# A fused attention and mixer kernel: the first 750 steps of the work issued in one written order on all five engines

## The chip, the cores and the metric

The kernel runs on one core of one Trainium2 chip. The metric is the device time of one execution in microseconds. The five engines that the text speaks of are PE (TensorE: matmuls and transposes), ACT (ScalarE), DVE (VectorE), POOL (GpSimd) and SP (SyncE, which only issues DMAs). Each works off its own instructions in the order in which they stand.

## The reference, cut to what matters

Linear attention over 8 batches, 8 heads, 576 tokens and 64 channels, and behind it a low-rank mixing over tokens and a two-layer MLP over channels, all in float32 accuracy. U, V, w_ch1 and w_ch2 arrive as float64.

```
phi(x):  proj = x @ w_phi                      # 64 -> 128
         proj -= max(abs(proj), axis=-1)
         return concat(exp(proj), exp(-proj))  # 256 features
q_p, k_p = phi(q), phi(k)
kv  = einsum('bhsf,bhsd->bhfd', k_p, v);  z = sum(k_p, axis=2)
x   = (q_p @ kv) / (q_p @ z + 1e-6)            # -> (8, 576, 512)
u   = x + ((x.T @ U) @ V).T                    # rank 32 over the 576 tokens
out = u + maximum(u @ w_ch1, 0) @ w_ch2        # 512 -> 2048 -> 512
```

## The kernel before, in words

**Pairs.** Attention is done in 32 pairs, (b, j), each two heads of a batch b, 512 tokens in the main part and 64 in a tail. A pair loads raw k and q (256 KB each) and the values, transposes both on PE (tiles T and tT), copies them from PSUM on ACT (T, tail_T; L393 to L399), multiplies by w_phi (pk and pkt for k, pq for q), forms the features (a maximum on DVE for k, on POOL for q, a subtraction on DVE, two exponentials on ACT), takes the kv product (36 matmuls into kv_ps, L549 and L559) and the output (xp, L577 and L584), and divides on DVE into x. From batch 2 on (pairs 8 and later) the operands are split into a rounded part and a remainder (`stack`, ACT L350 and DVE L351; pkt at L471), and w_phi is split into w_hl (L100 and L101).

**Tokens.** When a batch's four pairs are done, x is split into xs (ACT L656, DVE L657), multiplied by U into pp (`down`, L670), by V into vp (`up`, L686) and added to x, which is stored. U and V are converted from float64 in the kernel (u_st, v_st).

**Mixers.** There are eight mixers, one for each batch, and a ninth for the tails. A mixer transposes u (pt, L702) and splits it into uT_hi and uT_lo (L280 and L281), and then does 34 chunks: `hidden(f)` is 12 matmuls (L717) and a relu on ACT, `add(f)` is 4 matmuls in mixer 0 and 12 in the others (L748). One hidden chunk stands ahead of its add.

**Weights.** w_ch1 and w_ch2 come as 32 blocks of 512 KB of float64 words. A block is loaded by SP into one of four staging buffers (tag "wide", NW = 4) and converted to float32 by ACT (L141 and L147) and DVE: a mask (L144), a shift (L149), a combination (L152) and a join (L156). The mask, the shift and the combination read the staging buffer; after the last of them and ACT's L141 the buffer is free for a later load. A block of w_ch1 is then split into w_hi (ACT, L239) and w_lo (DVE, L246); those of w_ch2 are split in mixer 1, where they are first needed in two parts (`split_w2`, ACT L255 and DVE L256).

**The order around the change.** `early()` writes out the eight pairs of batches 0 and 1, the tokens of batch 0 and mixer 0, in the order of its code, helper by helper. A pair's step such as `whole_k` issues its matmuls, its DVE and its ACT instructions in one piece; `uv` converts U and V in four pieces; `conv(n)` converts n blocks; `chunk(n, blocks)` issues n chunks of mixer 0 and so many blocks. Mixer 0 has 23 of its chunks in `early()`. `keep_busy(n)` issues n matmuls of zeros (28 in all). PE, ACT, DVE and POOL follow this order; SP's is made by the scheduler. After that `ordered()` goes on with the pairs, chunk by chunk, and there only PE's order is written.

Of the kernel before, what the change touches and what calls it, by code (L numbers as in the profile page):

```python
# [21 lines left out]
HP = 64  # L22


@with_exitstack
def tile_kernel(
# [66 lines left out]

    def split_w():

        if not w_split:
            src = wide("w_src", (F,))
            load_w_phi(src)
            w_hl = const.tile([P, 2, F], F32R, tag="w_phi", name="w_hl")
            nc.vector.tensor_copy(out=w_hl[:, 0, :], in_=src)  # L100
            nc.vector.tensor_sub(w_hl[:, 1, :], src, f32(w_hl[:, 0, :]))  # L101
            w_split.append(w_hl)
        return w_split[0], w_split[0][:, 0, :], w_split[0][:, 1, :]
# [31 lines left out]
    def convert(st, a, b_, between=None):  # L135

        n = st.shape[1]
        hi_w = st[:, :, 1]
        halves = st.rearrange("p n w -> p (n w)").bitcast(U16).rearrange("p (n h) -> p n h", h=4)
        bh = b_.bitcast(U16).rearrange("p (n h) -> p n h", h=2)  # L140
        nc.scalar.activation(out=bh[:, :, 0], in_=halves[:, :, 1], func=AF.Copy, scale=2.0 ** -13)  # L141
        if between is not None:
            between()
        nc.vector.tensor_scalar(  # L144
            out=bh[:, :, 1], in0=halves[:, :, 3], scalar1=0x7FF0, scalar2=None,
            op0=ALU.bitwise_and)
        nc.scalar.activation(  # L147
            out=bh[:, :, 1], in_=bh[:, :, 1], func=AF.Relu, scale=8.0, bias=e_bias)
        nc.vector.tensor_scalar(  # L149
            out=a, in0=hi_w, scalar1=3, scalar2=0x7FFFF8,  # L150
            op0=ALU.logical_shift_left, op1=ALU.bitwise_and)
        nc.vector.scalar_tensor_tensor(  # L152
            out=a, in0=hi_w, scalar=-0x80000000, in1=a, op0=ALU.bitwise_and, op1=ALU.bitwise_or)

    def join(a, b_):
        nc.vector.tensor_tensor(out=a, in0=a, in1=b_, op=ALU.add)  # L156

    def staged(name, n):

        t = wide(name, (512, 2), I32)  # L160
        a, b_ = (t[:, 256 + 128 * i:256 + 128 * (i + 1), :].rearrange("p n w -> p (n w)")[:, 0:n]
                 for i in range(2))

        def go():
            convert(t[:, 0:n, :], a, b_)
            join(a, b_)
            return f32(a)

        return t[:, 0:n, :], go

    def uv_parts():
        st, go = staged("u_st", (NT + 1) * R)
        sv = st.rearrange("p (t r) w -> p t r w", r=R)
        nc.sync.dma_start(
            out=sv[:, 0:NT], in_=U[0:SM].rearrange("(p t) r w -> p t r w", t=NT))
        for g in range(2):
            nc.sync.dma_start(out=sv[g * ST:(g + 1) * ST, NT], in_=U[SM:S])
        cs3 = (slice(0, SM // 2), slice(SM // 2, SM), slice(SM, S))  # L180
        v_st = []
        for cs in cs3:
            sv, sgo = staged(f"v_st{cs.start}", cs.stop - cs.start)
            for g in range(4):
                nc.sync.dma_start(out=sv[g * R:(g + 1) * R], in_=V[:, cs])
            v_st.append(sgo)
        yield
        u_f = go().rearrange("p (t r) -> p t r", r=R)
        nc.vector.memset(f32(u_all[:, NT:NT + 2]), 0.0)
# [3 lines left out]
        for pr, to, of in parts:  # L193
# [5 lines left out]
        for cs, go in zip(cs3, v_st):  # L199
            yield  # L200
            v_f = go()
            vm = v_all[:, cs]
            if cs.stop <= SM:
                ps_ = slice(cs.start // NT, cs.stop // NT)
                v_f = v_f.rearrange("r (p t) -> r t p", t=NT)
                vm = v_all[:, 0:SM].rearrange("r (t p) -> r t p", t=NT)[:, :, ps_]
            nc.vector.tensor_copy(out=vm, in_=v_f)
            lo = slice(3 * R, 4 * R)
            nc.vector.tensor_sub(vm[lo], v_f[lo], f32(vm[lo]))


# [3 lines left out]
    AHEAD = 4  # L215
    loaded, begun, ended = [], [], [0]

    def load_block():
        i = len(loaded)
        f, m = i // 2, i % 2 + 1  # L220
        fs = slice(f * P, (f + 1) * P)
        st = wide(f"w{m}_{f}", (C, 2), I32)
        if m == 1:
            nc.sync.dma_start(
                out=st.rearrange("p (c n) w -> p c n w", c=NCC),
                in_=w1[:, fs].rearrange("(c p) n w -> p c n w", c=NCC))
        else:
            nc.sync.dma_start(out=st, in_=w2[fs])
        loaded.append(st)
# [29 lines left out]
    def conv(n=1):  # L259

        for _ in range(n):
            while len(loaded) < min(len(begun) + AHEAD, NB):
                load_block()
            some = ended[0] < len(begun)
            if len(begun) < NB:
                i = len(begun)
                f, m = i // 2, i % 2 + 1
                at = NFC + (f + 1 if m == 2 else (f + 2) % (NFC + 1))
                b_ = const.tile([P, C], I32, tag=f"wh{m}_{f}", name=f"w_b{m}_{f}")
                r = const.tile([P, C], F32, tag=f"wl{at}", name=f"w_r{m}_{f}")  # L270
                convert(loaded[i], r.bitcast(I32), b_, merge_block if some else None)
                begun.append((f, m, b_, r))
            elif some:
                merge_block()
            if some:
                end_block()


    def split_t(src, dst_hi, dst_lo):
        nc.scalar.copy(out=dst_hi, in_=src)  # L280
        nc.vector.tensor_sub(dst_lo, src, f32(dst_hi))  # L281

# [7 lines left out]
    home_of = {("xs1", t): homes[t] for t in range(NT + 1)}  # L290
# [15 lines left out]
    class Pair:  # L306


        def __init__(self, b, j):
            self.b, self.h0, self.nm, self.par = b, 2 * j, f"{b}_{j}", j % 2  # L310
            self.split = b >= SPLIT
            self.free = b * NPAIR + j <= NPAIR
            self.tail = slice((b % 2) * ST, (b % 2 + 1) * ST)
            nm, hs = self.nm, slice(self.h0, self.h0 + 2)
            self.raw = []
            for n, src in enumerate((k, q)):
                if b == 0:
                    m = home(("raw", j, n), (2, NT // 2, 2 * D), f"raw{nm}_{n}")
                else:
                    m = raw.tile(  # L320
                        [P, 2, NT // 2, 2 * D], F32, tag="raw", bufs=2, name=f"raw{nm}_{n}")
                nc.sync.dma_start(
                    out=m.rearrange("p h s e -> p h (s e)"),
                    in_=src[b, hs, 0:SM, :].rearrange("h (p t) d -> p h (t d)", t=NT))
                self.raw.append(m)

            if b == 0:
                self.t_r = home(("t_r", j), (2 * D,), f"t_r{nm}")
            else:
                self.t_r = raw.tile([P, 2 * D], F32, tag="t_r", bufs=1, name=f"t_r{nm}")  # L330
# [5 lines left out]
        def ps(self, name, late=False):  # L336
            return ps(f"{name}{self.nm}", "o" if late and self.free else "at")
# [10 lines left out]
        def stack(self, src, dst):  # L348

            nc.scalar.copy(out=dst[0:D], in_=src)  # L350
            nc.vector.tensor_sub(dst[D:2 * D], src, f32(dst[0:D]))  # L351
# [13 lines left out]
        def transpose_both(self):  # L365
# [11 lines left out]
            self.pT = []  # L377
            for n in self.order():
# [9 lines left out]
        def order(self):  # L388
            return (1, 0) if self.b == 0 else (0, 1)
# [435 lines left out]
    def early(x, xt):  # L825
# [15 lines left out]
        for i in range(NPAIR - 1):  # L841
# [12 lines left out]
            if i == 2:  # L854
                tk.down(0)
# [184 lines left out]
```

## Time and profile before

| | us |
|---|---|
| median of 3 runs | 1186.24 |
| lowest and highest | 1183.31, 1186.37 |
| the profiled execution, its own time | 1184.01 |
| its span, first to last instruction | 1182.1 |
| PE busy in the span | 1134.0 (96%) |
| DVE busy | 655.9 (55%) |
| ACT busy | 531.9 (45%) |
| POOL busy | 153.5 (13%) |
| mean granted clock of TensorE | 0.982 |

1.9 us of the execution lie outside the span. The first hidden matmul of mixer 0 starts at 88.15 us, that of mixer 1 at 245.81. In a row of the timeline stand the start, the busy time, the engine, the line, the operation, the output and inputs without their numbers, and the count; in brackets the idle time of the engine before it and what ended that. In a row of the waits stand who waited, whom for, the total in us, the times and the longest.

### The profile page before, as it was taken

The numbers are of one execution on the slowest core, as the hardware profiler recorded it, in microseconds if no ns is written. First come the engines' busy times: TensorE is split into PE (matmuls) and PEld (weight loads), VectorE is DVE, ScalarE is ACT, GpSimd is POOL, SyncE is SP. The second block draws the span as 40 slices with busy tenths as digits, with TensorE's granted clock in tenths as the row PEclk, the third lists the DMA queues.
The fourth block names the chain that finished last, engine by engine and source line by source line (L and its number), as shares of the span: only waits on it lengthen the run. The fifth ranks groups of instructions, "written<-read, shape, count | busy, mean of one in ns | idle before, by whom it ended". The sixth has DMA issues, their size and how long they took to land.

```text
span 1182.1 us, 22322 instructions
## 1 busy us (share of the span) xinstructions
PE 1134.0 (96%) x9231; PEld 928.6 (79%) x9236; DVE 655.9 (55%) x1355; ACT 531.9 (45%) x1134; POOL 153.5 (13%) x119
## 2 busy tenths in 40 slices
PE   8759988999999999999999999999999999999997
PEld 5547655778888888888888888888888888888886
DVE  4788898666565556555565656655665535112111
ACT  7577876434454454345443545444444532111110
POOL 4210111101120111111110212011111110000000
PEclk9869998999999999999999999999999999999999
DMA  4345552221113112211122111311231003100001
GB/s 134 103 152 153 167 168 60 66 86 32 36 54 105 31 32 58 92 55 32 31 86 76 32 31 50 108 36 32 59 105 32 28 1 125 40 1 29 8 1 35
DMA packets 90532, 75.73 MB, mean 64 GB/s; under 512 B 51648, under 2 KB 76736, under 8 KB 90304
## 3 DMA queue, kind: packets, MB, share of 16 engines
q1 hardware_dynamic: 90432, 74.31, 20.8%
q8 instruction: 73, 1.20, 0.4%
q14 instruction: 27, 0.22, 0.1%
HBM read 55.41 MB, written 18.87 MB: 63 GB/s over the span
## 4 chain that ended last, share of the span: by engine, by line
PE 86%; DVE 8%; ACT 3%; issue 2%; DMA 1%; POOL 0%; SPq 0%; DVEq 0%; POOLq 0%; ACTq 0%
PE ph L717 31%; PE o L748 31%; PE kv_ps L559 5%; PE xp L584 4%; PE pk L519 2%; PE pp L670 2%; PE T L409 2%; PE pt L702 1%; PE kv_ps L549 1%; DVE w_r L156 1%; PE pq L540 1%; PE pq L541 1%; PE xp L577 1%; DVE w_r L152 1%; PE vp L686 1%
## 5 line engine op out<-in xcount | busy, mean ns | idle before, releaser
L717 PE MATMUL ph<-uT_hi,w_hi 128*128 128x512 f32 x576 | 232.3, 403 | 5.9 <-DVE h_lo L734 5.2
L734 DVE SCALAR_TENSOR_TENSOR h_lo<-ph,h_hi 128x512 fp32r<-128x512 f32 x128 | 88.3, 690 | 265.3 <-ACT h_hi L733 265.3
L717 PE MATMUL ph<-uT_lo,w_hi 128*128 128x512 f32 x576 | 225.9, 392 | 0.2 <-DVE uT_lo L281 0.2
L717 PE MATMUL ph<-uT_hi,w_lo 128*128 128x512 f32 x576 | 225.5, 391 | 0.0
L733 ACT ACTIVATE h_hi<-ph 128x512 fp32r<-128x512 f32 x128 | 76.3, 596 | 326.8 <-PE ph L717 326.3
L748 PE MATMUL o<-w_hi,h_hi 128*128 128x512 f32 x512 | 204.7, 400 | 0.0
L748 PE MATMUL o<-w_hi,h_lo 128*128 128x512 f32 x512 | 199.9, 390 | 0.0
L748 PE MATMUL o<-w_lo,h_hi 128*128 128x512 f32 x512 | 199.6, 390 | 0.0
L457 POOL PARTITION_ALL_REDUCE qp<-qp x64 | 126.7, 1992 | 180.2 <-ACT qp L456 179.6
L717 PEld LDWEIGHTS ph<-uT_hi,w_hi 128*128 128x128 f32 x576 | 108.9, 189 | 30.4 <-DVE h_lo L734 6.5
L717 PEld LDWEIGHTS ph<-uT_hi,w_lo 128*128 128x128 f32 x576 | 108.6, 188 | 23.9
L717 PEld LDWEIGHTS ph<-uT_lo,w_hi 128*128 128x128 f32 x576 | 108.8, 189 | 21.3 <-issue 0.7
L748 PEld LDWEIGHTS o<-w_hi,h_lo 128*128 128x128 f32 x512 | 96.1, 188 | 20.9
L748 PEld LDWEIGHTS o<-w_hi,h_hi 128*128 128x128 f32 x512 | 96.3, 188 | 18.2
L748 PEld LDWEIGHTS o<-w_lo,h_hi 128*128 128x128 f32 x512 | 96.4, 188 | 17.8
L457 POOL PARTITION_ALL_REDUCE qp_t<-qp_t x32 | 25.7, 804 | 630.6 <-ACT qp_t L456 630.6
L351 DVE TENSOR_TENSOR T<-T,T 64x512 fp32r<-64x512 f32 x96 | 66.1, 689 | 23.1 <-ACT T L350 21.1
L350 ACT CAST T<-T 64x512 fp32r<-64x512 f32 x96 | 55.8, 581 | 29.6 <-DVE T L351 19.5
L584 PE MATMUL xp<-kv,qp 128*64 128x65 f32 x2048 | 66.3, 224 | 0.0
L559 PE MATMUL kv_ps<-vb,kp 128*64 128x65 f32 x2048 | 65.8, 223 | 0.0
L559 PEld LDWEIGHTS kv_ps<-vb,kp 128*64 128x64 f32 x2048 | 64.9, 139 | 0.0
L584 PEld LDWEIGHTS xp<-kv,qp 128*64 128x64 f32 x2048 | 63.6, 140 | 0.0
(137 smaller groups left out, 1535.3 us busy)
## 6 DMA issues: line engine op xcount, KB each, us to landing
w<-in_moe_w_ch_dram SPq DMA_DIRECT2D x32, 512.0 KB, 3.8
raw<-in_k_dram SPq DMA_DIRECT2D x32, 256.0 KB, 3.0
raw<-in_q_dram SPq DMA_DIRECT2D x32, 256.0 KB, 2.7
vb<-in_v_dram SPq DMA_DIRECT2D x64, 128.0 KB, 2.9
u_dram<-x SPq DMA_DIRECT2D x32, 256.0 KB, 2.6
st<-u_dram SPq DMA_DIRECT2D x16, 512.0 KB, 3.8
out_dram<-st SPq DMA_DIRECT2D x32, 256.0 KB, 2.7
t_r<-in_k_dram SPq DMA_DIRECT2D x32, 32.0 KB, 2.2
```

Source lines behind the costliest of these rows:

```text
L350: nc.scalar.copy(out=dst[0:D], in_=src)
L351: nc.vector.tensor_sub(dst[D:2 * D], src, f32(dst[0:D]))
L409: nc.tensor.transpose(out=pT[:, c * P:(c + 1) * P], in_=self.raw[n][:, c // 2, c % 2, :], identity=ident)
L457: nc.gpsimd.partition_all_reduce(qp[0], qp[1], P, ReduceOp.absmax)
L519: nc.tensor.matmul(pk[:, i, :, :], self.T[0][:, i, cs], w_hl, start=True, stop=True)
L559: nc.tensor.matmul(self.kv_v[z * HP:(z + 1) * HP, f, g, :], kp[f][:, i, z * HP:(z + 1) * HP], self.vb[:, g, t, :], start=False, stop=(t == ...
L584: nc.tensor.matmul(xv[zs, c, :], qp[f][:, c * P + z * HP:c * P + (z + 1) * HP], self.kv[:, f, c // 2, :], start=(f == 0), stop=(f == 1), s ...
L670: nc.tensor.matmul(pp, lhs, xs[:, n, :], start=(t == 0 and n == 0), stop=(t == NT and n == 1))
L717: nc.tensor.matmul(ph, l[:, c * P:(c + 1) * P], r[:, c, :], start=(n == 0), stop=(n == len(terms) * NCC - 1))
L733: nc.scalar.activation(out=h_hi, in_=ph, func=AF.Relu)
L734: nc.vector.scalar_tensor_tensor(out=h_lo, in0=ph, scalar=0.0, in1=f32(h_hi), op0=ALU.max, op1=ALU.subtract)
L748: nc.tensor.matmul(self.o[t], l[:, cs], r, start=(f == 0 and n == 0), stop=(f == NFC - 1 and n == len(terms) - 1))
```

## The change

`early()` no longer calls the helpers one after the other. Each helper has a counterpart that describes its work as steps (`Pair.work`, `uv_work`, `weight_work`, `Tokens.half_work`, `transpose_k_work`): one step is one or a few instructions of one engine, with the steps that must be issued ahead of it and the buffers it takes and frees. About 727 steps are numbered in the order of description, and the table ORDER names them in the order in which they are issued; "*n" stands for keep_busy(n), a letter behind a number picks a PSUM bank, and what stands behind a "/" is issued behind a later chunk of the ordered part. What a step computes is unchanged. SP's instructions are steps too, so all five engines follow the table up to the last pair of the second batch. 22 chunks of mixer 0 stand in the early part, and 33 keep_busy matmuls. `ordered()` is as before. The diff, cut to its core:

```
+ORDER = """
+1 4 *8 5o 6 49 2 0 511 3 48 47 515 *1 7a 8 11oo 28ao 31 13 18 32 9o 512 10 46 54a *2 12a 52a
...
+class Work:
...
+    def add(self, engine, fn, after=(), take=(), free=()):
+        self.steps.append(Step(engine, fn, after, take))
+        return self.steps[-1]
+
+    def issue(self, n):
+        for word in ORDER.split("/")[n].split():
...
+            assert not step.done and all(a.done for a in step.after)
+            step.fn()
+            step.done = True
...
+        p0 = work.add("ACT", low, after, free=free)
+        p1 = work.add("DVE", mask, after, free=free)
+        p2 = work.add("ACT", size, (p1,))
+        p3 = work.add("DVE", shift, after, free=free)
+        return work.add("DVE", join, (p0, p2, p3))
...
-                if b == 0 or b == 1 and i == 0:
-                    xs = home((f"xs{b}", t), (2, C // 2), f"xs{b}_{i}_{t}", F32R)
...
-    def chunk(n=1, blocks=0):
...
-            if i == 1:
-                next(uv)
-                next(uv)
-                tk.split(0)
...
-        while ended[0] < NB:
-            conv()
...
+    CHUNKS = 22
+
+    def early(x0, xt):
+
+        w = Work(keep_busy)
...
+        for i in range(NPAIR):
+            p[i].work(
+                w, p[i - 1] if i > 0 else None, p[i - 2] if i > 1 else None, (),
+                lambda: xs[0], True, w_done)
+        u_done, v_done = uv_work(w)
...
+        w.issue(0)
...
     with tc.manual_schedule(
-            engines={e.engine for e in (nc.tensor, nc.scalar, nc.vector, nc.gpsimd)}):
+            engines={e.engine for e in (nc.tensor, nc.scalar, nc.vector, nc.gpsimd, nc.sync)}):
         cur, nxt, x, xt, tk = early(x, xt)
```

Line numbers in the pieces of order below are those of each kernel. First, ACT between the feature exponentials of pair (0,2) and the copies of T of pair (0,3): T_0_3 and tail_T_3 are that pair's transposes, u_st and v_st the staged U and V, xs the first split of x. Before:

```order
L443 ACTIVATE kp_2_11_552<-kp_2_11_552 128x512
L141 ACTIVATE u_st<-u_st 128x160
L147 ACTIVATE u_st<-u_st,warm 128x160
L141 ACTIVATE v_st_151<-v_st_151 128x256
L147 ACTIVATE v_st_151<-v_st_151,warm 128x256
L656 CAST xs_0_0_641<-x_111 128x256
L656 CAST xs_0_1_644<-x_111 128x256
L656 CAST xs_0_2_647<-x_111 128x256
L656 CAST xs_0_3_650<-x_111 128x256
L656 CAST xs_0_4_653<-xt_112 128x256
L393 COPY T_0_3_658<-T_0_3_660 128x512
L396 COPY tail_T_3_656<-tT_3_670 64x2x64 x2
```

After, where T of pair (0,3) is first copied and then again (L579):

```order
L651 ACTIVATE qp_1_t<-qp_1_t 128x128
L649 ACTIVATE qp_1_00_312<-qp_1_01_313 128x512
L651 ACTIVATE qp_1_01_313<-qp_1_01_313 128x512
L579 COPY T_0_3_417<-T_0_3_530 128x512
L619 COPY qp_2_t<-pqt_2_518 128x128
L619 COPY qp_2_01_608<-pq_0_2_520 128x512
L619 COPY qp_2_11_611<-pq_0_2_522 128x512
L649 ACTIVATE qp_1_10_420<-qp_1_11_421 128x512
L651 ACTIVATE kp_2_01_437<-kp_2_01_437 128x512
L649 ACTIVATE kp_2_10_449<-kp_2_11_450 128x512
L579 COPY T_0_3_418<-T_0_3_648 128x512
```

Before, the conversions of U and V and five casts of x stand in one piece ahead of the first T; now exponentials and copies of pairs (0,1) and (0,2) stand there, the conversions have gone to other places, and the casts of x too.

Second, DVE where pair 8 (T_2_0, tail_T of batch 2) is split. w_lo_0 to w_lo_3 are splits of w_ch2 (L256) that mixer 1 uses, w_b and w_r parts of a block's conversion. Before:

```order
L152 SCALAR_TENSOR_TENSOR w_r_15_2305<-w_15_2240,w_r_15_2305 128x512
L246 TENSOR_TENSOR w_lo_15_2314<-w_r_15_2297,w_hi_15_2308 128x512
L256 TENSOR_TENSOR w_lo_0_2723<-w_r_0_883,w_hi_0_2722 128x512
L351 TENSOR_TENSOR T_2_0_2326<-T_2_0_2321,T_2_0_2326 64x512
L256 TENSOR_TENSOR w_lo_1_2783<-w_r_1_1112,w_hi_1_2782 128x512
L256 TENSOR_TENSOR w_lo_2_2836<-w_r_2_1195,w_hi_2_2835 128x512
L351 TENSOR_TENSOR T_2_0_2326<-T_2_0_2321,T_2_0_2326 64x512
L351 TENSOR_TENSOR tail_T_0_2320<-tT_0_2318,tail_T_0_2320 64x2x64
L256 TENSOR_TENSOR w_lo_3_2969<-w_r_3_1327,w_hi_3_2968 128x512
L351 TENSOR_TENSOR tail_T_0_2320<-tT_0_2318,tail_T_0_2320 64x2x64
```

After (L231 is the mask, L240 the shift, L243 the combination, L248 the join, L364 w_lo of w_ch1, L471 the split of T and tail_T):

```order
L857 COPY kv_3_2349<-kv_ps_3_2169 128x260
L471 TENSOR_TENSOR T_2_0_2147<-T_2_0_2142,T_2_0_2147 64x512
L231 TENSOR_SCALAR w_b_14_2210<-w_14_2109 128x512
L243 SCALAR_TENSOR_TENSOR w_r_12_2351<-w_12_2158,w_r_12_2351 128x512
L248 ISA w_r_9_2028<-w_r_9_2028,w_b_9_1979 128x1024
L471 TENSOR_TENSOR tail_T_0_2141<-tT_0_2139,tail_T_0_2141 64x2x64
L231 TENSOR_SCALAR w_b_11_2234<-w_11_2167 128x512
L248 ISA w_r_14_2154<-w_r_14_2154,w_b_14_2210 128x1024
L364 TENSOR_TENSOR w_lo_12_2241<-w_r_12_1928,w_hi_12_2239 128x512
L471 TENSOR_TENSOR tail_T_0_2141<-tT_0_2139,tail_T_0_2141 64x2x64
L471 TENSOR_TENSOR T_2_0_2147<-T_2_0_2142,T_2_0_2147 64x512
```

Before, w_ch2's splits stand between the parts of pair 8's transposes; now the conversions of blocks stand there, and these splits come later. On PE, two hidden chunks and the kv product of the last pair now stand between pair 8's transposes and its pkt, where four o matmuls stood.

Third, DVE at the blocks of weights in the second batch, with numbers, since the names read alike without them: w1_6 is block 6 of w_ch1, w2_5 block 5 of w_ch2. Before:

```order
L144 TENSOR_SCALAR w_b1_6_1574<-w1_6_1397 128x512
L149 TENSOR_SCALAR w_r1_6_1575<-w1_6_1397 128x512
L152 SCALAR_TENSOR_TENSOR w_r1_6_1575<-w1_6_1397,w_r1_6_1575 128x512
L156 ISA w_r1_6_1575<-w_r1_6_1575,w_b1_6_1574 128x1024
L144 TENSOR_SCALAR w_b2_6_1584<-w2_6_1514 128x512
L149 TENSOR_SCALAR w_r2_6_1585<-w2_6_1514 128x512
L152 SCALAR_TENSOR_TENSOR w_r2_6_1585<-w2_6_1514,w_r2_6_1585 128x512
L246 TENSOR_TENSOR w_lo1_6_1594<-w_r1_6_1575,w_hi1_6_1588 128x512
L156 ISA w_r2_6_1585<-w_r2_6_1585,w_b2_6_1584 128x1024
```

After:

```order
L240 TENSOR_SCALAR w_r2_5_1662<-w2_5_1540 128x512
L243 SCALAR_TENSOR_TENSOR w_r2_5_1662<-w2_5_1540,w_r2_5_1662 128x512
L231 TENSOR_SCALAR w_b1_7_1671<-w1_7_1665 128x512
L248 ISA w_r2_3_1557<-w_r2_3_1557,w_b2_3_1514 128x1024
L248 ISA w_r2_4_1560<-w_r2_4_1560,w_b2_4_1538 128x1024
L231 TENSOR_SCALAR w_b1_8_1695<-w1_8_1685 128x512
L240 TENSOR_SCALAR w_r1_7_1702<-w1_7_1665 128x512
L243 SCALAR_TENSOR_TENSOR w_r1_7_1702<-w1_7_1665,w_r1_7_1702 128x512
L240 TENSOR_SCALAR w_r1_6_1708<-w1_6_1543 128x512
L243 SCALAR_TENSOR_TENSOR w_r1_6_1708<-w1_6_1543,w_r1_6_1708 128x512
L231 TENSOR_SCALAR w_b1_9_1715<-w1_9_1697 128x512
```

Before, the three reads of a block's staging buffer (mask, shift, combination) stand together; now the mask of a block stands ahead of other blocks' shifts and joins. The buffer that w2_5 leaves (its combination is the second row) is that which w1_9 is loaded into.

More of the change, by code (lines that the diff above doesn't have):

```diff
@@ L155, in join @@
[L155 to L189, printed above, removed]
@@ new lines, in staged, with begin, part @@
+    def staged(work, name, n, load, size):
+        s, got = Slot("wide"), []
+        def begin():
+            got.append(wide(name, (512, 2), I32))
+            load(got[0][:, 0:n, :])
+        def part(i):
+            t = got[0][:, 256 + 128 * i:256 + 128 * (i + 1), :]
+            return t.rearrange("p n w -> p (n w)")[:, 0:n]
+        ld = work.add("SP", begin, take=(s,))
+        j = convert(work, lambda: got[0][:, 0:n, :], lambda: part(0), lambda: part(1), (ld,), n, ())
+        return j, s, lambda: f32(part(0))
@@ L197, in uv_parts @@
                 nc.vector.tensor_copy(out=u_all[pr, to, i, :], in_=f32(u_all[pr, to, 0, :]))
[L199 to L209, printed above, removed]
+        last = ju
@@ new lines, in uv_work, with load_v, v_part @@
+        for n in range(3):
+            last = work.add(
+                "DVE", lambda n=n: u_part(n), (last,), free=(su,))
+        done = [last]
+        for cs in (slice(0, SM // 2), slice(SM // 2, SM), slice(SM, S)):
+            def load_v(st, cs=cs):
+                for g in range(4):
+                    nc.sync.dma_start(out=st[g * R:(g + 1) * R], in_=V[:, cs])
+            n = cs.stop - cs.start
+            jv, sv, v_src = staged(work, f"v_st{cs.start}", n, load_v, 4)
+            def v_part(cs=cs, v_src=v_src):
+                v_f = v_src()
+                vm = v_all[:, cs]
+                if cs.stop <= SM:
+                    ps_ = slice(cs.start // NT, cs.stop // NT)
+                    v_f = v_f.rearrange("r (p t) -> r t p", t=NT)
+                    vm = v_all[:, 0:SM].rearrange("r (t p) -> r t p", t=NT)[:, :, ps_]
+                nc.vector.tensor_copy(out=vm, in_=v_f)
+                lo = slice(3 * R, 4 * R)
+                nc.vector.tensor_sub(vm[lo], v_f[lo], f32(vm[lo]))
+            done.append(work.add("DVE", v_part, (jv,), free=(sv,)))
@@ L212, in tile_kernel @@
+        return done[0], done[1:]
     w_hi_t, w_lo_t, w_t = {}, {}, {}
     NB = 2 * NFC
[L215 to L229, printed above, removed]
@@ L257, in split_w2 @@
         w_hi_t[2, f], w_lo_t[2, f] = hi, lo
[L259 to L281, printed above, removed]
     SPLIT = 2
@@ L334, in __init__, with ps @@
                     in_=src[b, hs, SM:S, :].rearrange("h r d -> r h d"))
-        def ps(self, name, late=False):
-            return ps(f"{name}{self.nm}", "o" if late and self.free else "at")
+        def ps(self, name):
+            return ps(f"{name}{self.nm}")
         def load_v(self):
@@ new lines, in copy_t @@
+            def copy_t():
+                for g in range(2):
+                    r_ = slice(g * D, (g + 1) * D)
+                    nc.scalar.copy(
+                        out=self.tail_T[r_, :, r_],
+                        in_=got["tT"][r_, 0:2 * ST].rearrange("p (n r) -> p n r", n=2))
+            for n in order:
+                sl = bank()
+                a[n] = add("PE", lambda n=n, sl=sl: tr(n, sl), (ld[n], mt), (sl,), (s_raw[n],))
+                cp[n] = add(
+                    "ACT",
+                    lambda n=n: nc.scalar.copy(out=self.T[n], in_=got[f"T{n}_"]),
+                    (a[n], mt), free=(sl,))
@@ new lines, in work, with rows @@
+            sl = bank()
+            at_ = add("PE", lambda sl=sl: tr_t(sl), (ldt, mt), (sl,), (s_tr,))
+            ct = add("ACT", copy_t, (at_, mt), free=(sl,))
+            s_q = [Slot(f"q{pre}{r}") if b == 0 else Slot("feat") for r in range(2)]
+            s_qt = Slot(f"qt{pre}") if b == 0 else Slot("feat_t")
+            s_k = [Slot(f"k{pre}{r}") if b == 0 else Slot("feat") for r in range(2)]
+            s_kt = Slot(f"kt{pre}") if b == 0 else Slot("feat_t")
+            def rows(r):
+                return slice(r * D, (r + 1) * D)
@@ new lines, in pe_kt, with q_copy, q_of @@
+            def pe_kt(sl):
+                nc.tensor.matmul(
+                    tile_("pkt", sl)[:, 0:F], self.tail_T[:, 0, :], w_f, start=True, stop=True)
+            def q_copy(r, m):
+                pq = got["pqt" if r == "t" else f"pq{r}_"]
+                qp = self.q_tile(r, m)
+                nc.scalar.copy(out=qp[1], in_=pq[:, 0:m])
+                if r == "t":
+                    self.qpt = qp
+                else:
+                    self.qp[r] = qp
+            def q_of(r):
+                return self.qpt if r == "t" else self.qp[r]
@@ new lines, in q_work @@
+            def q_work(after):
+                sls = [bank(), bank()]
+                Q = add("PE", lambda: pe_q(sls), (cp[1], w_done, *q_room), sls, (s_T,))
+                slt = bank()
+                Qt = add("PE", lambda: pe_qt(slt), (ct, w_done, *q_room), (slt,), (s_T,))
+                qe = {}
+                last = None
+                for r in (0, 1, "t"):
+                    pe, sl, s_, m = (Qt, slt, s_qt, 2 * ST) if r == "t" else (Q, sls[r], s_q[r], SM)
+                    c = add(
+                        "ACT", lambda r=r, m=m: q_copy(r, m),
+                        (pe, *after, *([last] if last is not None and r != "t" else [])), (s_,),
+                        (sl,))
+                    if r != "t":
+                        last = c
+                    mx = add("POOL", lambda r=r: q_max(r), (c,))
+                    sb = add("DVE", lambda r=r: q_sub(r), (mx,))
+                    qe[r] = exps(r, q_of, sb)
+                return qe, Q, Qt
```

709 lines of the change are left out of this document (464 added, 245 removed), and 14 rows, old and new, of the table ORDER.

## Prediction

> **What bounds the kernel now.** I read the busy shares by stretch first. The stretches are cut at the first hidden matmul of mixer 0 (88 us), where the pairs of the second batch begin to thin out (191 us), and at the first hidden matmul of mixer 1 (246 us), after which the change touches nothing. The columns are the stretch, its length, and the busy time of PE, PEld, DVE, ACT and POOL with counts, then the granted clock, DMA share and GB/s.
>
> ```profile
> 4.00:88.00 84.00, 59.63 (x798) 46.47 (x803) 57.03 (x149) 57.08 (x125) 24.56 (x20) 0.82 0.45 130
> 88.00:191.00 103.00, 97.79 (x824) 66.11 (x824) 87.92 (x180) 82.92 (x150) 10.98 (x8) 0.98 0.50 154
> 191.00:246.00 55.00, 49.53 (x318) 33.96 (x316) 42.09 (x79) 27.95 (x59) 9.79 (x6) 0.94 0.19 60
> 246.00:1182.00 936.00, 924.35 (x7289) 781.35 (x7287) 468.02 (x946) 362.46 (x801) 106.47 (x69) 1.00 0.16 48
> ```
>
> From 246 us on PE is busy 924 of 936 us: TensorE bounds the kernel, and an earlier start of mixer 1 moves the end by as much. So the question is what the first 246 us can give back. PE is idle there for 84 − 59.63 = 24.4, 103 − 97.79 = 5.2 and 55 − 49.53 = 5.5 us, 35.1 in all. The granted clock adds to this: the six places where it fell to half follow, with the sum below.
>
> ```profile
> 36.94:47.18 10.24, 5.89 (x42) 3.49 (x44) 6.82 (x25) 7.23 (x19) 3.11 (x2) 0.50 0.37 115
> 60.84:71.08 10.24, 5.53 (x70) 5.11 (x72) 9.00 (x19) 8.87 (x18) 0.00 (x0) 0.50 0.68 216
> 74.50:81.32 6.82, 5.91 (x18) 3.92 (x19) 4.83 (x11) 3.58 (x11) 0.45 (x1) 0.50 0.25 77
> 84.74:88.15 3.41, 2.74 (x12) 2.33 (x12) 3.08 (x6) 2.39 (x5) 1.33 (x3) 0.50 0.92 312
> 170.07:173.48 3.41, 3.41 (x19) 2.91 (x19) 2.42 (x6) 2.44 (x5) 0.00 (x0) 0.50 0.74 257
> 200.79:207.61 6.82, 3.92 (x12) 3.43 (x13) 6.60 (x15) 3.75 (x11) 0.00 (x0) 0.50 0.00 0
> ```
>
> At half clock half of the busy time is extra: (5.89 + 5.53 + 5.91 + 2.74)/2 = 10.0 us before 88, 3.41/2 = 1.7 in the middle, 3.92/2 = 2.0 at the end. Idle and extra together are 34.4 us in stretch A (4 to 88), 6.9 in B (88 to 191) and 7.4 in C (191 to 246): 48.7 us is the most that any order could return.
>
> The waits of PE say where it went. Columns: who waited, for whom, us in total, times, longest; the last row is from 88:246.
>
> ```profile
> PE pkt L478 <- issue: 7.6, 1, 7.6
> PE pq L500 <- ACT T L393: 7.3, 2, 6.8
> PE pp L670 <- ACT xs L656: 3.2, 1, 3.2
> PE T L381 <- DMA raw<-in_q_dram: 2.1, 2, 1.8
> PE pt L702 <- DVE x L687: 2.0, 1, 2.0
> ...
> PE pkt L471 <- DVE tail_T L351: 5.4, 1, 5.4
> ```
>
> The reader is to see that in A the long waits are on ACT and DVE, which are themselves busy only 57 of 84 us: each engine works its rows in order, and a lump of work nobody needs yet stands ahead of the row that PE needs. Two rows of PE's timeline show the two ends of the first lump.
>
> ```profile
> 34.12 0.38 PE L800 MATMUL busy<-zeros 128*128 128x512 bf16 x1
> 41.29 1.22 PE L500 MATMUL pq<-T,w_f 64*128 64x512 f32 x2 [6.79 <-ACT T L393]
> ```
>
> In between ACT works off u_st, v_st and five xs casts, the rows of before's first piece above, and only then copies T. The 7.6 us put down to issue has the same shape: the last v_st and two weight blocks stand ahead of the next copies on ACT.
>
> ```profile
> 63.73 0.87 ACT L147 ACTIVATE w_b<-w_b,warm 128x512 uint16<-128x512 uint16 x1
> 64.93 0.52 ACT L396 COPY tail_T<-tT 64x128 f32<-64x128 f32 x2
> ```
>
> The pkt matmul that reads this tail_T starts at 65.55.
>
> **Stretch A.** The change spreads these lumps: the copy of T of pair (0,3) no longer stands behind them, and the first x split has left that place. How long A then takes is not shown by a row of its own, so I bound it by the rate of the busier engines, ACT and DVE (57.1 and 57.0 us of work, which the change reorders and keeps). In 4:88 they run at 57.08/84 = 0.68: at that rate nothing is gained. In B, with chunks filling PE, ACT runs at 82.92/103 = 0.81: A would take 57.08/0.805 = 70.9 us, a gain of 13.1. The nearest row is that of the pairs alone, ahead of the first lump:
>
> ```profile
> 4.00:34.00 30.00, 25.93 (x405) 20.32 (x408) 16.02 (x38) 22.81 (x51) 14.52 (x12) 1.00 0.50 137
> ```
>
> There ACT runs at 22.81/30 = 0.76 and the clock stays full. I take this rate: 57.08/0.76 = 75.1, a gain of **8.9 us** (0 to 13.1), half clock included.
>
> **Stretch B.** Before mixer 0's first hidden matmul the table also puts the kv product of pair (1,0), the transposes and k products of (1,1) and the output of (1,0). Their size, from these rows:
>
> ```profile
> 92.08 2.04 PE L559 MATMUL kv_ps<-vb,kp 128*64 128x65 f32 x64
> 169.48 0.46 PE L478 MATMUL pkt<-w_f,tail_T 128*128 128x128 f32 x2 [2.37 <-issue]
> 169.87 2.25 PE L483 MATMUL pk<-w_f,T 64*128 64x128 f32 x16
> L584 PE MATMUL xp<-kv,qp 128*64 128x65 f32 x2048 | 66.3, 224 | 0.0
> ```
>
> That is 2.0 for kv, 66.3/32 = 2.1 for the output, 2.7 for k (at half clock): about 6.8 us of PE work that leaves B and C and fills idle time of A, if ACT and DVE have its inputs ready there. I take half, **3.4 us** (0 to 6.8), because their own inputs are ACT and DVE rows that compete in A.
>
> The 2.37 us wait before 169.48 was followed by half clock from 170.07 to 173.48, with PE busy for all of it. The Trainium skill, "TensorE: Matmul & The Clock Gate", Part 1: The HAM clock gate, has half rate come after an idle window of about 3.4 us or more. By that rule this 2.4 us wait would have cost no half clock and B's 1.7 would have another cause; the row shows otherwise, at least that shorter waits can bring it, and the sum goes by the row.
>
> **Stretch C.** The 5.39 us wait is this on DVE:
>
> ```profile
> 194.04 1.25 DVE L100 CAST w_hl<-w_src 128x128 fp32r<-128x128 f32 x1
> 195.33 0.29 DVE L101 TENSOR_TENSOR w_hl<-w_src,w_hl 128x128 fp32r<-128x128 f32 x1
> 198.68 0.69 DVE L256 TENSOR_TENSOR w_lo<-w_r,w_hi 128x512 fp32r<-128x512 f32 x1
> 200.12 1.42 DVE L256 TENSOR_TENSOR w_lo<-w_r,w_hi 128x512 fp32r<-128x512 f32 x2
> 202.61 0.69 DVE L256 TENSOR_TENSOR w_lo<-w_r,w_hi 128x512 fp32r<-128x512 f32 x1
> 203.34 0.29 DVE L351 TENSOR_TENSOR tail_T<-tT,tail_T 64x128 fp32r<-64x128 f32 x1
> ```
>
> Four splits of w2 (0.69 + 1.42 + 0.69 = 2.80) and the split of w_phi (1.54) stand ahead of the tail_T that PE needs, 4.34 us. In after w_phi's split comes before pair 8's transposes and the w2 splits behind them. Rows of weight blocks take their place (the second pair of pieces above: two masks, a combination, two joins, a w_lo, about 3.8 us by the groups quoted below), but PE has work of its own there: a kv product (2.0) and 24 hidden matmuls, which at the mean of 924.35/7289 = 0.127 us take 3.0 at least, against that 3.8. I take 4.34 and the half clock, 2.0: **6.3 us**; the ends are 0 (another wait takes its place) and all 5.39 + 1.96 = 7.35. The w2 splits are done later, where DVE is busy 468 of 936 us; without that cover they cost their 2.8.
>
> **What it adds.** Five more keep_busy matmuls, by the row at 34.12 at most 5 × 0.38 = 1.9 us; where PE waits they cost nothing; I take **1.0**. DVE and ACT get slightly more rows ahead of mixer 0's first hidden matmul, together under a microsecond by the means of their groups, taken at **0.8** (0 to 1.6). The chunk that moves to the ordered part has the same 12 matmuls, so it costs nothing; if it lacked cover it would bring one more wait of the kind seen at the next mixers' starts:
>
> ```profile
> PE ph L717 <- DVE h_lo L734: 5.2, 6, 1.2
> ```
>
> that is, 1.2 us. The early part's SP issues are now written out too: no PE wait there but the 2.1 us for raw is for a load, so I cost it at nothing in the sum and as a rival below.
>
> Sum: 8.9 + 3.4 + 6.3 − 1.0 − 0.8 = 16.8 us. The profiled run took 1184.0 us with a span of 1182.1; the span becomes 1165.3 and that run 1167.2. The median of the three runs is 1186.24, the lowest 1183.31, so a median lies between 0.7 below and 2.2 above this run; with 0.8 more, **1168**. A measurement of this kernel tells about 0.3% (3.6 us) from no change.
>
> **Rivals.** *A runs as tightly as B* (chance 0.23): 13.1 + 6.8 + 7.35 − 1.8 = 25.4, so 1182.1 − 25.4 + 1.9 = 1158.6. For it: ACT and DVE reach 0.81 and 87.92/103 = 0.85 in B. Against it: in A the two feed each other within one pair, which B's chunks hide.
>
> *The order keeps the rates* (0.10): the chain through one pair sets A, not the place of the lumps, and another input is late in C. Then only the costs and at most half of C stay: 1182 to 1187. Against it is 0.76 in 4:34; for it, that no row shows a whole stretch A without lumps.
>
> *Weight blocks come late* (0.13), the one that ends slower. In before the mask, shift and combine of a block stand together, so its staging buffer comes free early; in after the three stand apart, and between the last read of w2_5 and the first read of w1_9, which takes its buffer, there stand only the rows of other blocks that the third pair of pieces above shows. These rows price them:
>
> ```profile
> L144 DVE TENSOR_SCALAR w_b<-w 128x512 uint16<-128x512 uint16 x26 | 12.3, 473 | 0.0
> L149 DVE TENSOR_SCALAR w_r<-w 128x512 int32<-128x512 int32 x26 | 11.9, 459 | 0.0
> L152 DVE SCALAR_TENSOR_TENSOR w_r<-w,w_r 128x512 int32<-128x512 int32 x26 | 18.0, 693 | 0.9
> L156 DVE CUSTOM_DVE_ANT_0 w_r<-w_r,w_b 128x1024 uint16<-128x1024 uint16 x26 | 18.8, 724 | 8.6 <-ACT w_b L147 7.6
> ...
> DMA to landing us min/median/max: 3.4/3.8/5.2
> ...
> 4.47 0.60 SPq L342 DMA_DIRECT2D vb<-in_v_dram  x1
> 5.11 0.63 SPq L345 DMA_DIRECT2D vt<-in_v_dram  x1
> ```
>
> Two masks, two joins, two shifts and two combines: 2 × (0.47 + 0.72 + 0.46 + 0.69) = 4.7 us. A load needs 3.8 to 5.2 from its issue, and four value issues ahead of it on SP another 2 × (0.60 + 0.63) = 2.5. So it lands 1.6 to 3.0 us late, and DVE, ACT and then PE stand. I count eight loads with so little work between in the order; at the upper end 8 × 3.0 = 24.0 us, over the 16.8 gained: 1167.2 + 24.0 = 1191. It decides from 16.8/8 = 2.1 us per load. Against it: in 88:191 DMA is busy only half of the time, and before shows no wait on a weight load. The Trainium skill, "TensorE: Matmul & The Clock Gate", the table's row on engine queue depth, gives VectorE, ScalarE and GpSimd strictly ordered queues: a late block would then hold all that stands behind it. The 5.39 us wait agrees with that.
>
> That the change doesn't do what it says is excluded by the pieces of order above: the steps do stand elsewhere.
>
> **Chances.** The forecast holds 0.54, the rivals 0.23, 0.10 and 0.13. Faster by over 0.3% is 0.54 + 0.23 = 0.77, within 0.10, slower 0.13. The forecast's own range is from the sum of its ends drawn in by half, some 1160 to 1177; the range to 8 in 10 takes in the tight case with its 1158.6 and a few us below, and the unchanged one: 1155 to 1187. It leaves out the late loads at their upper end.
>
> **What would show it.** In after's profile: mixer 1's first hidden matmul some 17 us earlier, at about 229 us; mixer 0's at about 80 (75.1 + 4 and the work moved ahead); ACT at 0.75 or more of stretch A; no PE wait over 3 us before mixer 1; no half clock in C. It would be wrong if DVE or ACT wait for DMA w, if PE keeps 20 us of idle time ahead of mixer 0, or if mixers 1 to 7 change by more than 2 us, since all my terms lie before them.

## The result, and the profile after

| | before | after |
|---|---|---|
| median, us | 1184.78 (4 runs) | 1146.63 (4 runs) |
| lowest and highest | 1183.27, 1186.37 | 1146.18, 1147.29 |
| profiled execution, its span | 1184.01, 1182.1 | 1147.03, 1145.2 |
| mean granted clock | 0.982 | 0.997 |

The ratio is 0.968, its 95% interval 0.966 to 0.970: 38 us faster. Forecast were 1168 and a range of 1155 to 1187. The sign was right and the size forecast less than half of what came, short even of the better rival (1158.6). So the question is which terms were too small, and which were missing.

The stretches of after, cut at its own first hidden matmuls of mixer 0 (74.8) and of mixer 1 (213.74), answer to the first fence of the prediction:

```profile
4.00:74.80 70.80, 59.89 (x973) 47.45 (x979) 64.89 (x155) 55.60 (x131) 25.76 (x19) 1.00 0.50 142
74.80:165.00 90.20, 89.93 (x664) 58.29 (x660) 81.89 (x168) 75.13 (x142) 16.12 (x11) 1.00 0.54 167
165.00:213.74 48.74, 46.32 (x305) 31.35 (x304) 43.01 (x84) 30.92 (x60) 5.42 (x3) 0.96 0.30 99
213.74:1145.20 931.46, 924.80 (x7294) 781.82 (x7292) 464.66 (x949) 362.64 (x801) 107.62 (x69) 1.00 0.16 49
```

Read with before's, PE's idle time fell in A from 24.4 to 10.9 us, in B from 5.2 to 0.3, in C from 5.5 to 2.4, and behind mixer 1's first hidden matmul from 11.7 to 6.7. Over the span it fell from 48.1 to 21.5 us, which is 26.6 of the 36.9 us. The other 10.3 are busy time (1134.0 to 1123.7): in this profile the half clock is gone but for one place near 200 us, and five more keep_busy matmuls are paid out of that. In A PE does 973 matmuls where it did 798, in 13.4 us less.

PE's waits in A of after (the first three rows), and from there to mixer 1:

```profile
PE xp L870 <- DVE kv L857: 3.0, 2, 2.2
PE vp L993 <- DVE pst L982: 2.9, 1, 2.9
PE xp L877 <- DVE kv L857: 1.5, 1, 1.5
...
PE vp L993 <- DVE pst L982: 2.4, 1, 2.4
PE o L1110 <- DVE w_r L248: 0.3, 1, 0.3
```

None of the long waits is left, and the longest of those that are left are all on DVE. DVE, which e7 below shows to bound A, has changed its rate: two windows of after show it.

```profile
4.00:34.00 30.00, 24.53 (x346) 18.54 (x349) 25.38 (x62) 23.02 (x56) 12.44 (x11) 1.00 0.65 184
34.00:74.80 40.80, 35.37 (x634) 28.92 (x635) 39.51 (x94) 32.57 (x76) 13.32 (x9) 1.00 0.39 110
```

DVE is the third busy figure: 25.4 us in the first 30, where it was 16.0 in before, and then 39.5 of 40.8 (0.97), where it was 41.0 of 54.15 (0.76). Over A it runs at 64.89/70.8 = 0.92.

### The profile page after: what moved, and what is told of

It reads as the page before. It is cut to its first block, busy times and chain, and to the rows that moved or that the text cites. A ratio compares the mean times of both kernels' runs of the same rounds, so it can differ in the third digit from the quotient of the medians.

```text
span 1145.2 us, 22290 instructions
## 1 busy us (share of the span) xinstructions
PE 1123.7 (98%) x9234; PEld 920.0 (80%) x9241; DVE 655.3 (57%) x1355; ACT 525.8 (46%) x1134; POOL 156.9 (14%) x119
## 4 chain that ended last, share of the span: by engine, by line
PE 90%; DVE 7%; DMA 1%; SPq 1%; issue 0%; ACT 0%; POOL 0%; DVEq 0%
PE o L1110 35%; PE ph L1079 33%; PE xp L877 5%; PE kv_ps L850 4%; PE pk L810 2%; PE T L732 2%; PE pp L969 1%; PE pt L1058 1%; DMA w<-in_moe_w_ch_dram 1%; PE kv_ps L840 1%; PE pq L831 1%; PE pq L832 1%; PE xp L870 1%; PE vp L993 1%; DVE kp L761 1%; DVE w_r L243 1%
## 5 line engine op out<-in xcount | busy, mean ns | idle before, releaser
L788 POOL PARTITION_ALL_REDUCE qp_t<-qp_t x24 | 17.7, 739 | 626.6 <-ACT qp_t L787 626.6
L788 POOL PARTITION_ALL_REDUCE qp<-qp x48 | 95.9, 1997 | 32.2 <-ACT qp L787 30.5
L471 DVE TENSOR_TENSOR T<-T,T 64x512 fp32r<-64x512 f32 x96 | 66.1, 689 | 29.6 <-ACT T L468 27.1
```

The lines of the kernel that those rows point to most:

```text
L788: nc.gpsimd.partition_all_reduce(qp[0], qp[1], P, ReduceOp.absmax)
```

## The experiments

Single runs of one kernel scatter: the changed kernel, run again later (e15), had a median of 1148.73 (1145.94 to 1149.5). I had expected 1146 to 1147.5 of it. Differences of 2 us between kernels measured apart are therefore not read. The start of mixer 0, which each run's profile shows once, scatters more: it is 74.80 in the first profile of the changed kernel and 77.70 in e15's, where the clock was at half from about 65 to 71.6 us (last section); e5 and e14, whose code is the same up to mixer 0, have 84.33 and 87.94. A start that differs by under 4 us therefore shows nothing by itself.

**The chunk (e1, e2).** In e1 the last `chunk(1, 2)` of before's early part is `conv(2)`. In e2 step 727, the 23rd chunk, stands at the end of the table's first segment, in place of the first "/", so that the words behind it keep their places between the chunks.

```
-        p[7].end_q()
-        chunk(1, 2)
+        p[7].end_q()
+        conv(2)
```
```
-CHUNKS = 22
+CHUNKS = 23
-... 634 635 652 646 / 656 440 ...
+... 634 635 652 646 727 656 440 ...
```

> The kernel before, with 22 chunks of mixer 0 in its early part; its order is otherwise its own. Phase theory: the 4.8 us that the changed kernel gains after mixer 1's first hidden matmul come from the one chunk that the ordered part does more, so the six waits of ph on h_lo (5.2 us together) go here too, and the time falls by 4 to 5 us, to about 1180. Rival: the waits hang on how far DVE is behind at the end of the early part, so they stay and the time is within 1 us of before.

> The changed kernel with 23 chunks in the early part, the step for the added chunk put at the end of the first segment of the table. Phase theory: the six waits of ph on h_lo come back, 4 to 5 us, about 1151; the first hidden matmul of mixer 1 stays within 1.5 us of 213.7. Rival: no waits come back, the time stays at 1146 to 1148.

e1: 1183.72, ratio 0.998 (0.996 to 1.000), not the 1180 expected. e2: 1160.24, 13.6 us above the changed kernel's first median and 11.5 above e15's, where I expected some 4 to 5. In e2 the waits on h_lo are back, six of them, and there is one wait on a weight block besides, since the added chunk's block is joined too late for it:

```profile
PE ph L1050 <- DVE h_lo L1067: 4.8, 6, 0.8
PE o L1081 <- DVE w_r L219: 4.2, 1, 4.2
```

In e1 no PE wait is left behind mixer 1's start, but the wait of pair 8's pkt has grown from 5.4 us by 4.0, which takes most of the gain back:

```profile
PE pkt L471 <- DVE tail_T L351: 9.4, 1, 9.4
```

So the phase theory holds for the waits, though neither time came as it said: one chunk more in the ordered part takes the six waits away, in either kernel. What it does is seen on PE at mixer 2. Hidden 0 and hidden 1 share one PSUM bank (the tag "ph" has one), and h_lo must have read hidden 0 out of it. In before, between the last row of hidden 0 (375.62) and the first of hidden 1 (377.49) stand only pkt and pk, up to 376.71; in after, six matmuls of an add stand behind pk as well, from 343.74 on. First before, then after:

```profile
375.62 0.39 PE L717 MATMUL ph<-uT_hi,w_lo 128*128 128x512 f32 x1
376.02 0.69 PE L519 MATMUL pk<-w_hl,T 128*128 128x256 f32 x4
377.49 0.50 PE L717 MATMUL ph<-uT_hi,w_hi 128*128 128x512 f32 x1 [0.78 <-DVE h_lo L734]
```
```profile
342.81 0.39 PE L1079 MATMUL ph<-uT_hi,w_lo 128*128 128x512 f32 x1
343.74 0.39 PE L1110 MATMUL o<-w_hi,h_hi 128*128 128x512 f32 x1
345.13 0.39 PE L1079 MATMUL ph<-uT_hi,w_hi 128*128 128x512 f32 x1
```

The shift lasts through all mixers, so 4.8 us come from a change of one chunk. That is not all of e2's loss. In its profile PE is idle 6.8 us more than in after's, with the 4.2 us wait among it, and busy 6.5 us more with the same matmuls, which is half clock; of that, e15, the changed kernel itself, has 3.8.

**Which engines need the table (e3, e4).** The engines under manual order in the early part are cut, to all but SP (e3, shown) and to PE alone (e4, where the set holds nc.tensor only).

```
-            engines={e.engine for e in (nc.tensor, nc.scalar, nc.vector, nc.gpsimd, nc.sync)}):
+            engines={e.engine for e in (nc.tensor, nc.scalar, nc.vector, nc.gpsimd)}):
```

> The changed kernel, with SP's instructions of the early part ordered by the scheduler instead of by the table. If SP's written order carries part of the gain, loads and stores stand in each other's way and DVE or ACT wait more for w: 3 to 8 us lost, 1150 to 1155. If it carries none, within 1 us of 1146.6.

> The changed kernel, where only PE follows the table in the early part, as in the ordered part, and the scheduler orders ACT, DVE, POOL and SP. Theory that the interleaving of ACT and DVE rows is what fills stretch A: most of the 22 us gained ahead of mixer 0 and in the work moved there are lost, 1160 to 1185. Rival, that PE's own order (work moved ahead, transposes earlier) carries the gain: 1147 to 1152.

e3: 1148.25 (1147.04 to 1149.96), within the scatter: SP's written order carries nothing that can be seen. e4: 1196.22, ratio to before 1.008 (1.006 to 1.010), beyond the range that I gave. PE's order alone is worse than the kernel before, and its stretch up to mixer 0 shows why:

```profile
4.00:108.79 104.79, 71.85 (x973) 56.21 (x979) 92.78 (x214) 83.64 (x175) 25.27 (x18) 0.85 0.58 170
```

The same 973 matmuls take 104.8 us, and DVE does 214 rows ahead of mixer 0 (92.8 us) instead of 155: the scheduler puts weight blocks there (17 combinations, L243, where after has 4), and PE waits up to 5.2 us for a kv copy on DVE and 8.1 us for a feature of k on ACT. PE's order alone does not bring the gain; it needs the order of ACT, DVE and POOL, which no run takes apart from each other.

**The lumps by hand (e5, e9).** In before, without a table: e5 puts each piece of the lumps behind the copies and products of a pair, e9 in addition the U and V pieces one to two pairs earlier. The edit of e5, cut:

```
             p[i + 1].copy_both()
             p[i + 1].whole_q()
+            if i == 1:
+                next(uv)
+            if i == 2:
+                tk.split(0)
...
             p[i + 1].whole_k()
+            if i > 0:
+                next(uv)
...
-            if i == 1:
-                next(uv)
-                next(uv)
-                tk.split(0)
```

> The kernel before, helper by helper, but with its lumps taken apart by hand: the pieces of the conversions of U and V, the first x split and the first weight blocks stand behind the copies of T that PE waits for, one piece at a place. No table. Theory that the lumps set stretch A (the step of the prediction): the 6.8 and 7.6 us waits of PE shrink below 3, mixer 0's first hidden matmul comes at 79 to 82 instead of 88, time 1175 to 1179. Rival, that DVE must be kept at work from the start and single rows must be interleaved: the waits come back at other places, A shrinks by under 3 us, time 1181 or more.

> The kernel before with the lumps taken apart as in the run before (e5), and the conversions of U and V two pairs earlier, inside the first two of the pairs, where DVE was busy only 16 of 30 us; the first weight block moves ahead as well. Theory that DVE's idle time at the start is what A can give back: mixer 0's first hidden matmul comes at 76 to 80 instead of 84.3 in e5, time 1174 to 1178. Rival, that only an order row by row can use that time: 82 or later, time 1180 or more.

e5: 1182.39, ratio 0.997 (0.995 to 0.999); mixer 0 starts at 84.33 instead of 88.15 (but at 87.94 in e14, with the same order up to there). e9: 1184.95, ratio 1.000 (0.999 to 1.001), mixer 0 at 87.47. In e5 the long waits on ACT's T are gone, and others have come (the first, second and fourth rows of its list; the first was not among before's rows):

```profile
PE xp L577 <- DVE kv L566: 7.4, 2, 4.3
PE pkt L471 <- DVE tail_T L351: 6.0, 1, 6.0
...
PE vp L686 <- DVE pst L674: 5.1, 1, 5.1
```

Taking the lumps apart helper by helper moves the wait from ACT to DVE and gains 3 us. DVE does 17.2 us in 4:34 in both e5 and e9, hardly more than before's 16.0: in these whole pieces its idle time at the start is not filled. By time both fall on the rival's side.

**DVE's idle start, undone within the table (e11).** 17 ACT and DVE steps of the conversions that stand ahead of pair (0,3)'s T are put there in one piece, with three loads that need their buffers (20 words of ORDER moved, nothing else).

> The changed kernel with the ACT and DVE rows of the conversions (U, the first part of V, two and a half weight blocks; some 10 us of DVE and 3.4 us of ACT) taken out of the first pairs and put in one piece ahead of the copy of T of pair (0,3), as in the kernel before; three loads that need their buffers follow them. If work for DVE in the first 30 us is what shortens A: 7 to 11 us lost, 1154 to 1158, with DVE busy under 18 of the first 30 us. If the gain of A lies elsewhere, under 3 us.

e11: 1150.73 (1149.7 to 1152.09): 2 to 4 us lost against the two medians of the changed kernel, less than the 7 to 11 I expected. DVE does 5.4 us less in the first 30 us, not as little as the 18 expected, and PE waits on it later:

```profile
4.00:34.00 30.00, 23.48 (x336) 17.86 (x337) 19.94 (x56) 20.43 (x49) 10.50 (x9) 0.98 0.59 163
```
```profile
PE xp L869 <- DVE kv L856: 5.9, 1, 5.9
```

Mixer 0 starts at 77.69, but so it does in e15 (77.70), with the order of the table: that A grew is not shown. DVE's early work is worth 2 to 4 us of the time at most, and is not what most of A's gain hangs on.

**Is A bound by DVE (e7, e8, e12, e16)?** e7 does ten 0.42 us subtractions twice; e8 moves batch 0's kv copies and V's rounding copies to ACT; e12 and e16 move V's copies and U's second and third copies to POOL. The edits of e7 and of e12:

```
+                if b == 0:
+                    nc.vector.tensor_sub(got[t][:, 1, :], src, f32(got[t][:, 0, :]))
                 nc.vector.tensor_sub(got[t][:, 1, :], src, f32(got[t][:, 0, :]))
```
```
-                nc.vector.tensor_copy(out=u_all[pr, to, i, :], in_=f32(u_all[pr, to, 0, :]))
+                nc.gpsimd.tensor_copy(out=u_all[pr, to, i, :], in_=f32(u_all[pr, to, 0, :]))
...
-                nc.vector.tensor_copy(out=vm, in_=v_f)
+                nc.gpsimd.tensor_copy(out=vm, in_=v_f)
```

> The changed kernel with the ten subtractions of batch 0's x split done twice: ten more DVE rows of 0.42 us, 4.2 us in all, ahead of mixer 0; nothing on PE or ACT. If DVE bounds stretch A (it is busy 39.5 of the last 40.8 us there), A and the time grow by 3 to 4.5 us, to 1150 to 1151. If the chain through ACT and PE does, under 1.5 us.

> The changed kernel with the kv copies of batch 0's pairs and the rounding copies of V moved from DVE to ACT: 4 x 0.42 + 3.8 = 5.5 us less on DVE in stretch A, as much more on ACT (55.6 to 61 of 70.8). If DVE bounds A, it shrinks by 2 to 4.5 us, time 1142 to 1145. If ACT then binds, or the copies of kv come later on ACT than on DVE, the time stays or grows: 1146 to 1150.

> The changed kernel with the rounding copies of V (3.8 us) and the second and third copies of U (1.5 us) on POOL, which is busy 25.8 of the 70.8 us of A, instead of DVE. If DVE bounds A and POOL's copies are no slower than three times DVE's: 2 to 5 us gained, 1142 to 1145. If they hold up POOL's reductions of q, or V comes later: 1146 to 1150.

> The changed kernel with the copies of U and V on POOL, as e12. If the 2.2 us by which mixer 0 started earlier reach the end: 1143.5 to 1145, 2 us below the changed kernel. If the end of the early part takes them back: within 1 us of it.

e7: 1152.33 (1151.57 to 1152.46), 3.6 to 5.7 us above the two medians of the changed kernel for 4.2 us of added DVE work, with mixer 0 at 80.61, later than in either of its profiles. PE waits for the rows that are done twice:

```profile
PE pp L969 <- DVE xs L1026: 3.9, 3, 1.7
```

So DVE binds A. e8: 1147.99, no gain: PE now waits for the kv copies on ACT.

```profile
PE xp L880 <- ACT kv L858: 2.5, 1, 2.5
PE vp L996 <- ACT kp_t L651: 2.5, 1, 2.5
PE xp L873 <- ACT kv L858: 1.6, 1, 1.6
```

e12: 1145.17. e16, the same kernel beside e15: 1144.76 (1144.25 to 1145.18) against 1148.73 (1145.94 to 1149.5). Mixer 0 starts at 72.56 and 72.05, 2.2 to 2.8 us earlier than in the changed kernel's first profile and 5.1 to 5.6 earlier than in e15's. All four runs of e16 lie below all five of e15, and below the changed kernel's first four; two of e12's four (1145.96 and 1146.99) do not. By median it is the fastest kernel measured here, by 2 to 4 us, with a ratio to before of 0.966 (0.963 to 0.968).

**The work ahead of mixer 0 (e10).** Nine steps are put behind the first hidden chunk: kv and output of pair (1,0), the k products of (1,1), and what follows from them (words of ORDER moved).

> The changed kernel with the kv product and the output of pair (1,0) and the k products of (1,1) put behind mixer 0's first hidden matmuls again, with the ACT and DVE rows that follow from them (nine steps of the table). If stretch A is bound by DVE, its idle PE time is filled by this work for free and the move back costs nearly all of its 6.8 us: 1151 to 1154. If PE, without that work, gets through A earlier, under 2 us: 1147 to 1149.

e10: 1154.1 (1151.85 to 1154.34). Mixer 0 starts at 73.95, 0.85 us ahead of the changed kernel's first profile and 3.75 ahead of e15's, and the end comes 5.4 to 7.5 us later. The clock was at half from about 67 us to 78.3, and 4.35 us of that lie behind mixer 0's start, so some 2.2 us of the loss are the clock's. In A this work is nearly free; behind it, it costs from half to all of the 6.8 us at which its length was estimated.

**keep_busy (e6).** All but the first eight are taken out of the table.

> The changed kernel without its keep_busy matmuls behind the first eight (25 fewer). If DVE sets stretch A, PE may run there at half clock without much loss: time 1146 to 1150, with half clock in several windows ahead of mixer 0. If PE's clock carries the gain, A grows by 5 us or more: 1152 to 1158.

e6: 1148.32 (1148.04 to 1150.51), within the scatter. PE's clock fell to half in two short places of A only (near 18 and 50 us); with the order of the table, these 25 matmuls of zeros are not what holds it up.

**Stretch C without the table (e13, e14).** As e1, and pair 8's first transposes two chunks earlier; e14 is e13 with e5.

```
             p[i].whole_q()
+            if i == 7:
+                p[8].transpose_k()
             chunk(1, 2)
...
-        p[8].transpose_k()
         p[7].end_q()
-        chunk(1, 2)
+        conv(2)
```

> The kernel before with 22 chunks in the early part and pair 8's first transposes and splits two chunks earlier, so that DVE does the splits of T and tail_T ahead of the first splits of w_ch2; nothing else is moved. Theory: the waits of ph on h_lo go (4.8 us) and so does the wait of pkt on tail_T with its half clock (7.4 us): 11 to 12 us, 1172 to 1175. Rival, that another wait takes its place there: 1178 to 1181.

> As e13, and with the lumps of the first batch taken apart as in e5. If the two gains are independent: 3 us below e13, 1169 to 1172. What is left to the changed kernel, some 23 to 26 us, is then the row-by-row order in stretches A and B and the work moved ahead of mixer 0. If they are not, within 1 us of e13.

e13: 1175.97, ratio 0.992 (0.990 to 0.994). It lies between the two expectations. The waits on h_lo are gone, that on tail_T is down from 9.4 us in e1 to 0.9, and 7.8 us lie between the medians of e1 and e13: that is what C's wait is worth, with most of its half clock (a 2.2 us wait for kv_ps and a short half clock near 211 us are new). e14: 1174.34, ratio 0.991 (0.989 to 0.993), above the 1169 to 1172 expected; the 1.6 us below e13 can't be told from nothing. Three edits by hand so bring 8 to 10 of the 38 us. The other 28 came with the table only; that they need an order row by row is not shown, since only these coarser orders were tried, and none of them moved the work of e10 ahead of mixer 0.

## Why the prediction was wrong, point by point

**What bounds the kernel** held: 32 of the 36.9 us of span came from the stretches ahead of mixer 1's first hidden matmul. Idle time and half clock together, in us, by stretch and against the terms of the sum:

| | before | after | returned | forecast |
|---|---|---|---|---|
| A | 34.4 | 10.9 | 23.5 | 8.9 and 3.4 |
| B | 6.9 | 0.3 | 6.6 | none |
| C | 7.4 | 4.0 | 3.4 | 6.3 |
| behind mixer 1's first hidden matmul | 11.7 | 6.7 | 5.0 | none |
| what the change adds | | | −1.9 (estimate) | −1.8 |

Half clock counts at half of the busy time in it, as in the prediction; in after that is 3.22/2 = 1.6 us in C and nothing elsewhere. The 1.9 are five more matmuls of zeros at 0.38. The forecast is 16.8, and the measured column adds up to 36.6 of the span's 36.9. B and C are cut at other places of the work in after than in before; together they returned 10.0 against 6.3. The term that was most in error is A's, by 11.2 us, and two stretches that returned 11.6 us had no term at all.

**Stretch A** had a step wrong and not only a size: it took ACT as the engine whose rate A can reach, 0.76 in 4:34, with ACT's 0.81 in B as the end of the range. DVE binds A in the changed kernel (e7). It ran at 57.0/84 = 0.68 in before, with 16.0/30 = 0.53 in 4:34 and 0.76 from there to mixer 0, and runs at 0.92 in after. A's 70.8 us match the end of the range, 70.9, by luck: the working has 57 us of ACT there, and what happened is 64.9 us of DVE at a higher rate. That the lumps stand ahead of T is true, but e5 and e9 show that taking them apart in whole pieces moves the wait to DVE and gains 3 us at most. The work moved ahead of mixer 0, taken at half of 6.8, cost 5.4 to 7.5 us when it was moved back (e10), some 2.2 of them the clock's: the half is the least that it was worth. I also charged 0.8 us for rows moved ahead of mixer 0; DVE did 7.8 us more by that point (64.9 against 57.0), and A was still shorter, since DVE had idle time to fill. There is little of that left: e7's added rows cost their length.

**"Costs nothing" for the moved chunk** failed. It returned 4.8 us behind mixer 1, where I had said that the change touches nothing; that the mixers behind change by over 2 us was one of my own signs of being wrong. The row of the six waits on h_lo was in the prediction; I read it as a price, not as something that a shift by one chunk could take away. e1 and e2 show it from both sides.

**Stretch B** got no term, though I had listed its 6.9 us of idle time and half clock; after has 0.3 us idle and full clock there. No run takes B apart from the rest.

**Stretch C**: the wait that was forecast to go did go, and e13 against e1 puts it at 7.8 us, where PE's wait was longer than in before (9.4 against 5.4); the forecast was 6.3. But in after C returned 3.4, because another wait took its place in part, 2.4 us of vp on pst, with half clock behind it. That is what the lower end of the term named, and "no half clock in C" failed.

**keep_busy** at 1.0 us and **SP's order** at nothing can't be refuted: e6 and e3 lie within the scatter.

**The rivals.** *A as tightly as B* was the right side, and its 25.4 us fell short for the same missing terms. *Late weight blocks* did come about, and cost little: from 74 us on, the longest wait of DVE on a block was 3.0 us, and PE had other work meanwhile.

```profile
DVE w_b L231 <- DMA w<-in_moe_w_ch_dram: 3.0, 1, 3.0
```

Only one PE wait of 0.3 us followed. *The order keeps the rates* was wrong for the table, and is near to right for e9.

What stays open: of A's 13.4 us and the work that it took in, e10 accounts for the moved work, e11 for 2 to 4 us at most and e6 for none that can be seen; the rest was not taken apart step by step, and is only known not to come from PE's order alone (e4).

## What to carry to other kernels

Where several engines feed each other and PE waits, look for the engine that is idle early and full later, and hold the stretch against its total work, not against the rate of the engine that PE happens to wait for; then add a known dose of work to that engine to see whether it binds. List every idle microsecond that you count as recoverable against a term of the sum: what has no term is a forecast of no gain. A shift of one step against a periodic order repeats in each period, so even a small one must be followed past the place of the edit. Before a few microseconds in a variant's profile are read, profile the unchanged kernel twice.

## What the runs showed of the hardware

Half clock came after short waits: in after, the one place at half clock follows a single wait of 2.4 us. The window, and PE's row ahead of it:

```profile
197.40:200.80 3.40, 3.22 (x5) 1.83 (x6) 3.30 (x6) 1.63 (x3) 0.00 (x0) 0.51 0.76 253
```
```profile
197.58 1.22 PE L993 MATMUL vp<-pst,v_all 128*128 128x512 f32 x2 [2.42 <-DVE pst L982]
```

A wait of that length did not always bring it. The same five matmuls of A stand behind a wait of 2.87 us in after's profile and of 2.84 us in e15's, which is the same kernel; in the one they took 1.42 us, in the other 2.50. First after, then e15, each row with its window:

```profile
65.50 1.42 PE L993 MATMUL vp<-pst,v_all 128*128 128x512 f32 x5 [2.87 <-DVE pst L982]
65.10:71.60 6.50, 6.10 (x97) 5.29 (x99) 6.44 (x14) 4.38 (x10) 0.02 (x1) 1.00 0.59 200
```
```profile
65.69 2.50 PE L993 MATMUL vp<-pst,v_all 128*128 128x512 f32 x5 [2.84 <-DVE pst L982]
65.10:71.60 6.50, 5.91 (x61) 4.86 (x63) 5.51 (x10) 2.81 (x6) 0.22 (x1) 0.50 0.68 221
```

In that window PE did 97 matmuls at full clock and 61 at half, and mixer 0 then starts 2.9 us later. What decides between the two is not shown.
